# Squares of the first weights on ScalarE, the first root on VectorE, and the third weights a third of a unit later, in an attention, FFT and MLP kernel on one core

## The chip, the core and the metric

The kernel runs on one core of one Trainium2 chip. The metric is device time in microseconds (us), the median of several executions. The engines of the core work in parallel, each through its own queue and in order: TensorE (PE, matmuls), VectorE (DVE), ScalarE (ACT), GpSimd (POOL) and SyncE (SP), whose queue issues the DMA transfers. A wait at the head of a queue holds up everything behind it on that engine.

## The reference: what is computed

```python
x = attn_out.transpose(0, 2, 1, 3).reshape(4, 576, 512)       # 8 heads of 64
X = np.fft.fft(np.fft.fft(x, axis=1), axis=2)
u = x + np.real(X)
un = (u - u.mean(-1, keepdims=True)) / np.sqrt(u.var(-1, keepdims=True) + 1e-6)
x = u + np.maximum(un @ w_ch1, 0.0) @ w_ch2                   # 512 -> 2048 -> 512
gate_pre = sum(conv_w[k] * xp[:, k:k + 576, :] for k in range(5))   # xp: x with 4 zeros ahead
out = (1 / (1 + np.exp(-gate_pre)) * (x @ w_val)) @ w_out
```

attn_out is the sum of two attentions over q, k, v (4 batches, 8 heads, 576 tokens, 64 wide): one over tokens averaged by fours, and one over a band of width |i-j| < 4. The five weight arrays come as 64-bit floats.

## The kernel before, in words

**Units.** The MLP and the gated convolution run over 12 units (b, j): batch b, and 192 of its 576 tokens, j = 0 to 2. A unit is `ln` (layernorm, lines 960 to 1033), `ph` (first product, L1106, 192 matmuls in 8 groups of 24), `hh` and `hl` (the f16 high and low half of the ReLU, by ACT L1110 and DVE L166), `pc` (second product, L1126, again 192), then five taps of the convolution (`W<-X,cw` or `tap<-X,cw`), `val` (the product with w_val, L1218), `gl` and `gh` (gate times value in two halves) and `out` (L1234). Products use three f16 passes: high by high, high by low, low by high. Only unit (0,0) is done in fp32 (L1068 and L1081), because the f16 halves of the weights do not exist yet.

**Weights.** A 64-bit weight arrives as two 32-bit words and is made an f32 by three integer operations on DVE (`to_f32`, lines L302 and L166; "words" below). The sum of squares of the array then gives a power of two as its scale (`pow2`), and `conv_w` makes a high half on ACT (L372) and a low half on DVE (L166, 128x1024). w_ch1 is `W1` (8 positions), w_ch2 is `W2` (8 positions), and w_val and w_out are the "third weights" (positions 16 to 19). The sum of squares of W1 comes from 64 bf16 matmuls of a block with itself (`gram`, L356), whose diagonal DVE adds up (`tr`, `ss`); for w_val it is squares on ACT and matmuls with ones (`cv`, L400), for w_out again a gram (`cv`, L356). The third weights' words arrive in tiles named `raw`, in slots that the attention of the next batch uses too; SP issues these transfers among the loads `v` of that attention, which wait for POOL's sums `vr` and `ptv`.

**Fourier.** While units (0,1) and (0,2) run, batch 1's attention and Fourier transform are done beside them: `ab` over features, `pp`, `pn` and `pq` over the sequence, the last of which DVE turns into `DS` and adds to X. Unit (1,0) starts with `ln(1,0)`, which needs these sums: `uc` (X less its mean), `sq`, the sum `st`, `vv`, the root `r` (seven operations), `uc<-uc,r`, and `uh` and `ul`, the f16 halves which `ph` reads.

**Order.** Every step is recorded with a position in units (`put`, `spread`; positions S_..., P_... in lines 52 to 80), some with a priority (`urgent`), and a scheduler then writes one queue for each engine. The changed constants are S_W1B (the last two W1 words), S_W3 (the third weights), P_T0 (taps, values and outputs of unit (0,0)) and ROOT_G (the units whose root is done by POOL). The root of the first unit is computed in `ln` (L1008 to L1025).

Of the kernel before, what the change touches and what calls it, by code (L numbers as in the profile page):

```python
# [51 lines left out]
S_W1B = -7.47  # L52
# [8 lines left out]
S_W3 = (1.02, 1.6)  # L61
# [6 lines left out]
P_T0 = ((0.4, 0.75), (0.8, 1.0), (1.3, 1.75))  # L68
# [11 lines left out]
ROOT_G = ((0, 0), (0, 1))  # L80
# [48 lines left out]
def attn_moe_kernel(ctx, tc, q_t, k_t, v_t, w1, w2, w_val, conv_t, w_out, c_feat, c_seq, c_band, c_eye, out):  # L129
# [121 lines left out]
    def total(cols, n, name, act=False):  # L251

        ps = pst("tot", [P, n])
        T.matmul(out=ps, lhsT=ones, rhs=cols, start=True, stop=True)
        if act:
            assert n == 1
            r = keep.tile([P, 1], F32, name="f2s_" + name)
            A.activation(out=r, in_=ps, func=AF.Copy, scale=float(DM))
            return r
        t = keep.tile([P, 1], F32, name="f2_" + name)  # L260
        V.tensor_reduce(out=t, in_=ps, axis=AX.X, op=ALU.add)
        r = keep.tile([P, 1], F32, name="f2s_" + name)
        V.tensor_scalar(out=r, in0=t, scalar1=float(DM), scalar2=None, op0=ALU.mult)
        return r
# [62 lines left out]
    def word_w(i):  # L327
        if i < 16:
            raw = raws.pop(i)
            n = 1024 // len(raw)  # L330
            pos = AT[i] if i < 8 else 8
            for z, x in enumerate(raw):
                last = to_f32(W[AT[i] + 1].bitcast(I32)[:, z * n:(z + 1) * n], x,
                       lambda g=gates if pos < 4 else gates1 if pos < 6 else gates2: g.pop(0) if len(g) > 1 else g[0])
            if pos == 7:
                gates2[:] = [last.ins]
            if i == 11:
                st[0]["worded"] = last
# [27 lines left out]
    def trace_w(key):  # L366
        return total(diagonal(gram[key], key), 1, key, key in ("w1", "w2"))
# [50 lines left out]
    def attn_steps(b):  # L418
# [63 lines left out]
        def dense(sp):  # L482
# [92 lines left out]
            def values(g, e):  # L575
# [37 lines left out]
                if not first:  # L613
                    A.activation(out=vw[g], in_=vw[g], func=AF.Square, accum_out=d["ssv"][:, g:g + 1])
# [61 lines left out]


# [8 lines left out]
        def lowres():  # L686
# [3 lines left out]

            for a in range(H // 2):
# [282 lines left out]
    def ln(b, j):  # L974
# [39 lines left out]
        r1 = tiny.tile([P, UT], F32, tag="r1", name="r1", bufs=2)
        for a, c in ((-0.703952253, 0.703952253 * 2.38924456), (-0.5, 1.5)):
            mul(e, r1, r0, r0)
            if e is G:
                mul(e, r1, r1, vv)
                e.tensor_scalar(out=r1, in0=r1, scalar1=a, scalar2=c, op0=ALU.mult, op1=ALU.add)
                mul(e, r0, r0, r1)  # L1020
            else:
                stt(e, r1, r1, a, vv, ALU.mult, ALU.mult)
                stt(e, r0, r1, c, r0, ALU.add, ALU.mult)
# [304 lines left out]
    def put(pos, f):  # L1328
        events.append((pos, len(events), f))
# [12 lines left out]
    put(S_G1[1], lambda: urgent(w1_scale, "S"))  # L1342
    spread([(1.0, lambda i=i: sumsq_w(i, "w2", i == 8, i == 15)) for i in range(8, 16)], *S_G2)
# [18 lines left out]
    assert S_N0 < S_W1B <= S_W2[0] and 4 / 17 < S_C0[0] and 8 / 17 < S_C1[0] and S_C1[1] <= 9 / 17  # L1362
# [81 lines left out]
```

## Time and profile before

| what | value |
|---|---|
| median of 3 runs | 730.36 us (728.93 to 731.26) |
| profiled execution | 730.66 us, of which the span of the trace is 728.9 us |
| PE busy | 687.0 us (94%) |
| DVE busy | 467.0 us (64%) |
| ACT busy | 316.9 us (43%) |
| POOL busy | 122.5 us (17%) |
| mean granted TensorE clock | 0.967 of full speed |

Times of the trace count from the first instruction of the span; 1.76 us of the profiled execution lie outside it. A line of the trace gives start, duration, engine, source line, operation, output and input tiles and shapes, and in brackets how long the engine stood idle before and what released it. Shares of busy time are averages over the whole span; what a stage can gain is read from the waits of that stage.

### The profile page before, as it was taken

The page shows a single profiled execution, that of the slowest core. Times are in us where ns is not written, and L with a number is a line of the kernel's source. Part 1 is how long each engine was busy: PE and PEld are TensorE (multiplying, and loading weights), DVE is VectorE, ACT ScalarE, POOL GpSimd, SP SyncE. Part 2 cuts the span into 40 slices and gives each one's busy share as a digit, 9 for nine tenths or more (in the row PEclk, how much of TensorE's full clock was granted, in tenths as well). Part 3 has the DMA queues.
Part 4 walks back from the last instruction along what each step waited for, and adds up shares of the span by engine and source line. Part 5 has one row for each costly group of instructions (what it writes and reads, how often), then busy time and mean ns, then how long its engine had stood idle before and what let it go on. Part 6 is the DMA issues. An engine that isn't in the chain of part 4 may idle for free.

```text
span 728.9 us, 18440 instructions
## 1 busy us (share of the span) xinstructions
PE 687.0 (94%) x7849; PEld 599.6 (82%) x7849; DVE 467.0 (64%) x978; ACT 316.9 (43%) x980; POOL 122.5 (17%) x167
## 2 busy tenths in 40 slices
PE   8588799989899988999999999999999999999997
PEld 4346599988778967868898898789899989999895
DVE  4885699987978776466976725829635572633324
ACT  1674224686355336756423835644413232322212
POOL 0400054025222022330202107003100010000000
PEclk9758999989999999999999999999999999999999
DMA  9964314623422301240230001003000000000001
GB/s 240 377 228 167 101 66 167 155 82 129 144 60 83 100 1 39 61 136 16 77 103 2 26 15 43 17 1 97 18 16 16 1 16 16 1 17 2 30 2 44
DMA packets 27574, 53.01 MB, mean 73 GB/s; under 512 B 2112, under 2 KB 16320, under 8 KB 26468
## 3 DMA queue, kind: packets, MB, share of 16 engines
q1 hardware_dynamic: 27492, 51.84, 22.1%
q8 instruction: 61, 1.00, 0.6%
q14 instruction: 21, 0.17, 0.1%
HBM read 45.34 MB, written 8.26 MB: 74 GB/s over the span
## 4 chain that ended last, share of the span: by engine, by line
PE 67%; DVE 18%; ACT 6%; DMA 5%; POOL 2%; issue 1%; SPq 1%; POOLq 0%; ACTq 0%; DVEq 0%
PE pc L1126 19%; PE ph L1106 18%; DVE W L166 6%; PE out L1234 5%; PE val L1218 5%; ACT dP L565 3%; DMA v<-in_v_dram 2%; PE po L751 2%; PE ab L863 1%; DVE fF L835 1%; PE dO L606 1%; PE ph L1068 1%; DVE X L172 1%; PE sc L701 1%; PE pc L1081 1%
## 5 line engine op out<-in xcount | busy, mean ns | idle before, releaser
L1106 PE MATMUL ph<-uh,W 128*128 128x192 f16 x1408 | 195.3, 246 | 1.6 <-ACT uh L1032 1.6
L1106 PEld LDWEIGHTS <-W 128*128 128x128 f16 x2112 | 175.1, 98 | 7.9 <-issue 6.4
L1106 PE MATMUL ph<-ul,W 128*128 128x192 f16 x704 | 173.2, 246 | 0.0
L1126 PE MATMUL pc<-hh,W 128*128 128x192 f16 x1232 | 171.6, 247 | 0.9 <-ACT hh L1110 0.9
L1126 PEld LDWEIGHTS <-W 128*128 128x128 f16 x1848 | 154.2, 98 | 10.4 <-issue 8.4
L1126 PE MATMUL pc<-hl,W 128*128 128x192 f16 x616 | 151.3, 247 | 3.9 <-DVE hl L166 3.9
L166 DVE SCALAR_TENSOR_TENSOR hl<-ph,hh 128x384 f16<-128x384 f32 x88 | 48.2, 550 | 91.3 <-ACT hh L1110 91.2
L1110 ACT ACTIVATE hh<-ph 128x384 f16<-128x384 f32 x88 | 43.1, 494 | 103.0 <-PE ph L1106 99.9
L166 DVE SCALAR_TENSOR_TENSOR W<-X,cw,W 128x192 f32<-128x192 f32 x160 | 60.2, 432 | 0.9 <-ACT W L1181 0.7
L1218 PE MATMUL val<-yy,W 128*128 128x192 f16 x576 | 52.9, 246 | 0.1
L1218 PEld LDWEIGHTS <-W 128*128 128x128 f16 x576 | 47.9, 98 | 2.4 <-issue 0.6
L565 ACT ACTIVATE dP<-dS,dmx 128x64 f32<-128x64 f32 x160 | 48.1, 337 | 0.7 <-PE dPT L586 0.3
L1234 PE MATMUL out<-W,gh 128*128 128x512 f16 x144 | 45.6, 379 | 0.0
L565 ACT ACTIVATION_READ_ACCUMULATOR dP<-dS,dmx 128x1 f32 x160 | 36.8, 230 | 0.0
L166 DVE SCALAR_TENSOR_TENSOR W<-W,W 128x1024 int32<-128x1024 int32 x24 | 29.0, 1232 | 0.1
L715 ACT ACTIVATE E<-sc,nm 72x144 f32<-72x144 f32 x64 | 23.6, 378 | 9.4 <-POOL vr L172 4.7
L1234 PE MATMUL out<-W,gl 128*128 128x512 f16 x72 | 27.3, 379 | 0.0
L1081 PE MATMUL pc<-h,W 128*128 128x192 f32 x128 | 26.2, 357 | 0.0
L1234 PEld LDWEIGHTS <-gh 128*128 128x128 f16 x144 | 14.1, 98 | 13.7 <-issue 0.2
L1126 PE MATMUL pc<-hh,Wz 128*128 128x192 f16 x176 | 25.2, 246 | 0.0
L1068 PE MATMUL ph<-u,W 128*128 128x192 f32 x128 | 24.0, 345 | 1.0 <-DVE u L996 1.0
L1126 PEld LDWEIGHTS <-Wz 128*128 128x128 f16 x264 | 22.2, 98 | 2.7 <-issue 0.2
(243 smaller groups left out, 1208.1 us busy)
## 6 DMA issues: line engine op xcount, KB each, us to landing
W<-in_moe_w_ch_dram SPq DMA_DIRECT2D x12, 1024.0 KB
v<-in_v_dram SPq DMA_DIRECT2D x32, 144.0 KB
out_dram<-osb SPq DMA_DIRECT2D x17, 256.0 KB
vw<-in_v_dram SPq DMA_DIRECT2D x16, 256.0 KB
X<-in_q_dram SPq DMA_DIRECT2D x6, 576.0 KB
kT<-in_k_dram SPq DMA_DIRECT2D x4, 582.0 KB
X<-in_moe_w_ch_dram SPq DMA_DIRECT2D x2, 1024.0 KB
raw<-in_moe_w_ch_dram SPq DMA_DIRECT2D x4, 512.0 KB
```

Source lines behind the costliest of these rows:

```text
L166: return eng.scalar_tensor_tensor(out=out, in0=in0, scalar=scalar, in1=in1, op0=op0, op1=op1)
L172: return eng.tensor_tensor(out=out, in0=a, in1=b, op=ALU.add)
L565: A.activation(out=s_[:, z, a], in_=pss[par][:, z, a], func=AF.Exp, scale=SCALE, bias=mx[:, par, z, a:a + 1], accum_out=su[:, par, z, a:a ...
L715: A.activation(out=E[:, qc], in_=ps[:, qc], func=AF.Exp, scale=SCALE / 16, bias=nm[:, qc:qc + 1], accum_out=su[:, qc:qc + 1],)
L751: T.matmul(out=po[par * 64:par * 64 + 64], lhsT=d["vr"][:, kc, (a % 2) * 4 + (a // 2) * 2 + par], rhs=ets[par][:, kc], start=(kc == 0), st ...
L1068: i = T.matmul(out=ps[:, e], lhsT=W[AT[kc * 2 + m // 8] + 1][:, o:o + 128], rhs=u()[:, kc, :], start=(kc == 0), stop=(kc == 3))
L1081: T.matmul(out=c["ps"][m // 2][:, m % 2], lhsT=W[9 + g][:, o:o + 128], rhs=hs[g // 2][:, g % 2, e, :], start=(kk == 0 and m % 2 == 0), sto ...
L1106: T.matmul(out=ps[:, e], lhsT=w1_ap(pw, kc, 2 * g + e), rhs=uh[px][:, kc, :], start=(t == 0), stop=(t == 11))
L1110: A.activation(out=h_, in_=ps, func=AF.Relu)
L1126: T.matmul(out=ps[m // 2][:, m % 2], lhsT=w2_ap(pw, kk, m), rhs=x[px][:, e, :], start=(kk == 0 and (pw, px) == (0, 0) and m % 2 == 0), sto ...
L1218: T.matmul(out=ps[:, e], lhsT=wv_ap(pw, kc, 2 * mh + e), rhs=m_["y"][px][:, kc, :], start=(t == 0), stop=(t == 11))
L1234: T.matmul(out=ps, lhsT=(gh, gl)[px][:, kc, t * 128:(t + 1) * 128], rhs=wo_ap(pw, kc), start=(n == 0), stop=(n == 11))
```

## The change

- W1's last two word positions are no longer recorded at S_W1B, after the first unit's mean is subtracted, but with the other six.
- W1's sum of squares is taken by eight ACT activations with an accumulated output, right behind `sq` of unit (0,0), in place of 64 gram matmuls, and its total adds eight columns.
- The first unit's root is done by DVE, recorded at S_R0 = 0.8, in place of POOL.
- The third weights are recorded at 1.35 to 1.95 in place of 1.02 to 1.6, and unit (0,0)'s taps, values and outputs about a third of a unit later.
- The squares of v (`vw`) of batches 1 to 3 are recorded in another function; their place in ACT's queue is in effect the same.

```diff
-S_W1B = -7.47
-S_W3 = (1.02, 1.6)
+S_W3 = (1.35, 1.95)
-P_T0 = ((0.4, 0.75), (0.8, 1.0), (1.3, 1.75))
+P_T0 = ((0.75, 0.93), (1.0, 1.3), (1.6, 2.0))
-ROOT_G = ((0, 0), (0, 1))
+ROOT_G = ((0, 1),)
+S_R0 = 0.8
...
 def total(cols, n, name, act=False):
...
-            assert n == 1
             r = keep.tile([P, 1], F32, name="f2s_" + name)
-            A.activation(out=r, in_=ps, func=AF.Copy, scale=float(DM))
+            A.activation(out=tiny.tile([P, n], F32, tag="p2t", name="p2t"), in_=ps, func=AF.Copy, scale=float(DM), accum_out=r)
...
 def word_w(i):
...
-                       lambda g=gates if pos < 4 else gates1 if pos < 6 else gates2: g.pop(0) if len(g) > 1 else g[0])
-            if pos == 7:
-                gates2[:] = [last.ins]
+                       lambda g=gates if pos < 4 else gates1 if pos < 8 else gates2: g.pop(0) if len(g) > 1 else g[0])
...
 def sumsq_w(i, key, first, last):
+        if key == "w1":
+            if first:
+                gram[key] = keep.tile([P, 8], F32, name="ss_" + key)
+            behind(st[0]["sq"].ins, lambda: A.activation(
+                out=spare.bitcast(BF16)[:, 0:1024], in_=W[AT[i] + 1], func=AF.Square,
+                accum_out=gram[key][:, i % 8:i % 8 + 1]))
+            return
...
-            behind(st[0]["st2"].ins if i < 8 else None, lambda: T.matmul(
-                out=gram[key], lhsT=blk, rhs=blk, start=(first and c == 0), stop=(last and c == 7)))
+            T.matmul(out=gram[key], lhsT=blk, rhs=blk, start=(first and c == 0), stop=(last and c == 7))
...
 def ln(b, j):
...
-        vv = tiny.tile([P, UT], F32, tag="r2", name="vv", bufs=2)
+        vv = tiny.tile([P, UT], F32, tag="r2", name="vv", bufs=2) if not head else keep.tile([P, UT], F32, name="vv0")
         e = G if (b, j) in ROOT_G else V
...
+        if head:
+            st[0]["r"], st[0]["root"] = r0, root
+            return
+        root()
...
+    put(S_R0, lambda: st[0]["root"]())
-    for r, f, p in ((W1_ORDER[:6], w_in, S_W1), (W1_ORDER[:4], w_out_, S_C0), (W1_ORDER[4:], w_out_, S_C1), (range(8, 16), w_in2, S_W2)):
+    for r, f, p in ((W1_ORDER, w_in, S_W1), (W1_ORDER[:4], w_out_, S_C0), (W1_ORDER[4:], w_out_, S_C1), (range(8, 16), w_in2, S_W2)):
-    for i in W1_ORDER[6:]:
-        put(S_W1B, lambda i=i: urgent(lambda: w_in(i), "S"))
```

The table of positions tells little of the queues, so three places are shown as the scheduler wrote them. Numbers behind a name tell buffers of one tile apart.

DVE, in unit (0,1): the words of the third weights (`W_122<-raw`, `W_123<-raw`) stand between the steps of the unit; `hl` at the end is the low half that the third group of the second product waits for. Before, from the operation that reads the second `raw` tile:

```order
L302 TENSOR_SCALAR W_122<-raw 128x512
L720 RECIPROCAL lsu<-lsu 72x2 x2
L166 SCALAR_TENSOR_TENSOR W_122<-raw,W_122 128x512
L708 TENSOR_REDUCE nm<-sc 72x2
L166 SCALAR_TENSOR_TENSOR W_122<-raw,W_122 128x512
L302 TENSOR_SCALAR W_122<-raw 128x512
L172 TENSOR_TENSOR sq<-sq 128x384
L708 TENSOR_REDUCE nm<-sc 72x2
L166 SCALAR_TENSOR_TENSOR W_122<-raw,W_122 128x512
L166 SCALAR_TENSOR_TENSOR hl<-ph,hh 128x384
```

With the change, from the same operation:

```order
L301 TENSOR_SCALAR W_122<-raw 128x512
L731 TENSOR_SCALAR lsu<-lsu 72x2
L732 RECIPROCAL lsu<-lsu 72x2
L166 SCALAR_TENSOR_TENSOR W_122<-raw,W_122 128x512
L732 RECIPROCAL lsu<-lsu 72x2
L166 SCALAR_TENSOR_TENSOR hl<-ph,hh 128x384
```

Three operations on raw words, two maxima `nm` and a sum `sq` that stood ahead of `hl` now stand behind it.

SP's queue at the same place: `v` are loads for batch 1's attention. Before:

```order
L189 DMA raw<-in_moe_w_val_dram 128x1024
L187 DMA v_1828<-in_v_dram 72x2x256
L189 DMA v_1863<-in_v_dram 72x2x256
L189 DMA v_1864<-in_v_dram 72x2x256
L189 DMA v_1871<-in_v_dram 72x2x256
L189 DMA v_1872<-in_v_dram 72x2x256
L189 DMA raw<-in_moe_w_val_dram 128x1024 x2
```

With the change:

```order
L189 DMA raw<-in_moe_w_val_dram 128x1024
L187 DMA v_1765<-in_v_dram 72x2x256
L189 DMA v_1800<-in_v_dram 72x2x256
L189 DMA v_1801<-in_v_dram 72x2x256
L189 DMA v_1808<-in_v_dram 72x2x256
L189 DMA raw<-in_moe_w_val_dram 128x1024
L189 DMA v_1809<-in_v_dram 72x2x256
L189 DMA raw<-in_moe_w_val_dram 128x1024
```

The second `raw` now stands ahead of the last of these loads.

DVE, at the start of unit (1,0), from the last sums of batch 1's Fourier part on. Before, the whole way to `uc<-X,st` and `sq`:

```order
L166 SCALAR_TENSOR_TENSOR DS<-pp,ivx_1_2033,qs 128x289 x2
L172 TENSOR_TENSOR X<-X,DS 128x289 x2
L172 TENSOR_TENSOR uc<-X 128x384
L172 TENSOR_TENSOR uc<-uc 128x192
L166 SCALAR_TENSOR_TENSOR X<-pc_3087,iv_1559,X 128x2x192
L996 TENSOR_TENSOR uc<-X,st 128x768
L554 TENSOR_REDUCE dmx<-dS 128x4 x2
L166 SCALAR_TENSOR_TENSOR X<-pc_3088,iv_1559,X 128x2x192
L172 TENSOR_TENSOR sq<-sq 128x384
L172 TENSOR_TENSOR sq<-sq 128x192
```

With the change, two pieces of the same stretch:

```order
L166 SCALAR_TENSOR_TENSOR DS<-pp,ivx_1_1970,qs 128x289 x2
L172 TENSOR_TENSOR X<-X,DS 128x289 x2
L166 SCALAR_TENSOR_TENSOR W_121<-W_122,s_wv,W_121 128x1024
L169 TENSOR_TENSOR tr<-cv,eye 128x128
L172 TENSOR_TENSOR uc<-X 128x384
L166 SCALAR_TENSOR_TENSOR W_121<-W_122,s_wv,W_121 128x1024
L366 TENSOR_REDUCE ss_wo<-tr 128x1
L172 TENSOR_TENSOR uc<-uc 128x192
```

```order
L166 SCALAR_TENSOR_TENSOR W_123<-X,cw,W_123 128x192 x2
L166 SCALAR_TENSOR_TENSOR gl<-tap,gh 128x2x192
L166 SCALAR_TENSOR_TENSOR W_123<-X,cw,W_123 128x192
L166 SCALAR_TENSOR_TENSOR tap<-tap,val 128x384
L166 SCALAR_TENSOR_TENSOR W_123<-X,cw,W_123 128x192
L169 TENSOR_TENSOR uc<-uc,r_2955 128x768
L166 SCALAR_TENSOR_TENSOR W_123<-X,cw,W_123 128x192 x4
L559 TENSOR_REDUCE dmx<-dS 128x8 x2
L166 SCALAR_TENSOR_TENSOR gl<-tap,gh 128x2x192
L166 SCALAR_TENSOR_TENSOR W_123<-X,cw,W_123 128x192 x2
L1050 TENSOR_TENSOR ul<-uc,uh 128x768
```

The conversions of w_val (and, between the two pieces, the trace, the scale and the two conversions of w_out), unit (0,0)'s two products `tap<-tap,val` and its two `gl`, and 13 taps of unit (0,1) stood ahead of `DS` before, and now stand between `DS` and `ul`. The two `X<-pc` that stood there are ahead of `DS` now, and `yy<-X`, which stood ahead of `ul`, too.

## Rows read from the trace of the kernel before

**Rows 1.** Stretches: bounds, us; busy (x count) PE, PEld, DVE, ACT, POOL; clock, DMA.

```profile
91.40:150.00 58.60, 58.43 (x583) 56.14 (x587) 57.91 (x79) 26.11 (x81) 19.80 (x25) 0.97 0.42 125
150.00:163.70 13.70, 11.50 (x151) 10.57 (x139) 10.40 (x18) 13.13 (x42) 2.33 (x6) 0.75 0.27 89
186.90:262.50 75.60, 74.23 (x810) 66.18 (x810) 59.00 (x141) 33.23 (x87) 12.69 (x18) 0.98 0.28 87
262.50:277.60 15.10, 10.56 (x164) 7.61 (x162) 13.29 (x25) 6.31 (x23) 4.54 (x6) 1.00 0.05 19
400.00:728.90 328.90, 323.69 (x3728) 294.76 (x3725) 167.84 (x387) 117.84 (x312) 32.55 (x42) 1.00 0.06 21
```

**Rows 2.** Timeline of PE, unit (0,0): start, us, line, operation, count, idle before.

```profile
99.80 3.83 PE L356 MATMUL gram<-W 128*128 128x128 bf16 x64
...
153.25 1.11 PE L606 MATMUL dO<-PT,vw 64*64 64x58 f32 x16 [2.20 <-ACT PT L592]
154.29 6.55 PE L1081 MATMUL pc<-h,W 128*128 128x192 f32 x22
...
161.85 1.89 PE L1081 MATMUL pc<-h,W 128*128 128x192 f32 x10
```

**Rows 3.** One line's instructions, L614 on ACT: min/median/max ns.

```profile
L614 ACT ACTIVATE vw<-vw x9: 628/1058/1161, 145.9 to 447.0; 128x1024 f32<-128x1024 f32 x6, 128x512 f32<-128x512 f32 x3
```

**Rows 4.** Timeline of DVE: base sums, and W1's last two words.

```profile
64.69 2.76 DVE L172 TENSOR_TENSOR X<-X,base 128x576 f32<-128x576 f32 x4 [8.67 <-ACT X L612]
...
92.58 4.62 DVE L166 SCALAR_TENSOR_TENSOR W<-W,W 128x1024 int32<-128x1024 int32 x4
```

**Rows 5.** Timeline of SP, loads between the first and second raw tile.

```profile
166.80 10.03 SPq L189 DMA_DIRECT2D v<-in_v_dram  x4
```

**Rows 6.** Timeline of DVE, the second raw tile and the third hl.

```profile
181.51 0.81 DVE L302 TENSOR_SCALAR W<-raw 128x512 int32<-128x512 int32 x1 [3.13 <-DMA raw<-in_moe_w_val_dram]
...
186.28 0.54 DVE L166 SCALAR_TENSOR_TENSOR hl<-ph,hh 128x384 f16<-128x384 f32 x1
```

**Rows 7.** Timeline of PE at the same place.

```profile
186.87 0.24 PE L1126 MATMUL pc<-hl,W 128*128 128x192 f16 x1 [2.56 <-DVE hl L166]
```

**Rows 8.** Timeline of DVE: what the change moves, where it stood.

```profile
222.86 1.30 DVE L166 SCALAR_TENSOR_TENSOR W<-W,s_wv,W 128x1024 f16<-128x1024 f32 x1 [1.62 <-ACT W L372]
...
228.94 0.14 DVE L248 TENSOR_SCALAR s_wo<-p2b 128x1 int32<-128x1 int32 x1
...
229.80 1.01 DVE L166 SCALAR_TENSOR_TENSOR tap<-tap,val 128x384 f32<-128x384 f32 x2
...
236.15 0.54 DVE L166 SCALAR_TENSOR_TENSOR gl<-tap,gh 128x384 f16<-128x384 f32 x1
...
293.06 2.74 DVE L166 SCALAR_TENSOR_TENSOR W<-X,cw,W 128x192 f32<-128x192 f32 x8
```

**Rows 9.** Timeline of DVE, end of ln(1,0).

```profile
266.64 0.61 DVE L166 SCALAR_TENSOR_TENSOR X<-pc,iv,X 128x384 f32<-128x384 f32 x1
...
276.61 1.01 DVE L166 SCALAR_TENSOR_TENSOR yy<-X,s_y,yy 128x768 f16<-128x768 f32 x1
277.60 0.96 DVE L1033 TENSOR_TENSOR ul<-uc,uh 128x768 f16<-128x768 f32 x1
278.48 1.28 DVE L554 TENSOR_REDUCE dmx<-dS 128x8 f32<-128x512 f32 x2
```

**Rows 10.** Timeline of PE: last pq, st, 12 out, first ph with ul.

```profile
262.23 0.29 PE L888 MATMUL pq<-seq,AL 96*128 96x289 f16 x1
...
270.55 0.56 PE L990 MATMUL st<-sq,ones 128*128 128x192 f32 x2 [2.49 <-DVE sq L172]
270.95 0.38 PE L1234 MATMUL out<-W,gh 128*128 128x512 f16 x1
...
273.33 0.38 PE L1234 MATMUL out<-W,gh 128*128 128x512 f16 x1
...
279.68 0.25 PE L1106 MATMUL ph<-ul,W 128*128 128x192 f16 x1
```

More of the change, by code (lines that the diff above doesn't have):

```diff
@@ L366, in trace_w @@
     def trace_w(key):
-        return total(diagonal(gram[key], key), 1, key, key in ("w1", "w2"))
+        if key == "w1":
+            return total(gram[key], 8, key, True)
+        return total(diagonal(gram[key], key), 1, key, key == "w2")
     def conv_w(i, s, eng):
@@ L612, in values @@
                     A.activation(out=X[:, x, :, PAD + q0:PAD + q0 + nt], in_=pos[x], func=AF.Copy)
-                if not first:
-                    A.activation(out=vw[g], in_=vw[g], func=AF.Square, accum_out=d["ssv"][:, g:g + 1])
             def pool_qk(z, w):
@@ L675, in dense, with squares @@
             steps.extend(lr + v1)
+            def squares():
+                for g in range(len(GROUPS)):
+                    A.activation(out=vw[g], in_=vw[g], func=AF.Square, accum_out=d["ssv"][:, g:g + 1])
+            if not first:
+                d["squares"] = squares
         def scale_x():
@@ L689, in _ @@
                 d["base"] = sm.tile([P, 4, SD], F32, tag="base", name="base", bufs=1)
+            if b:
+                steps.append((0.1, d["squares"]))
             for a in range(H // 2):
@@ L1001, in ln @@
         sq = l_t("sq", [P, 4, UT])
-        A.activation(out=sq, in_=uc, func=AF.Square)
+        i = A.activation(out=sq, in_=uc, func=AF.Square)
+        if head:
+            st[0]["sq"] = i
         ps = colsum(sq, sq)
-        vv = tiny.tile([P, UT], F32, tag="r2", name="vv", bufs=2)
+        vv = tiny.tile([P, UT], F32, tag="r2", name="vv", bufs=2) if not head else keep.tile([P, UT], F32, name="vv0")
         e = G if (b, j) in ROOT_G else V
-        if e is G:
+        if e is G or head:
             A.activation(out=vv, in_=ps, func=AF.Copy, bias=1e-6)
@@ L1011, in ln, with root @@
         r0 = keep.tile([P, UT], F32, name="r00") if head else tiny.tile([P, UT], F32, tag="r0", name="r0", bufs=2)
-        e.tensor_scalar(out=r0.bitcast(I32), in0=vv.bitcast(I32), scalar1=-0.5, scalar2=float(0x5F1FFFF9),
-                        op0=ALU.mult, op1=ALU.add)
         r1 = tiny.tile([P, UT], F32, tag="r1", name="r1", bufs=2)
[L1015 to L1023, printed above, removed]
+        def root():
+            e.tensor_scalar(out=r0.bitcast(I32), in0=vv.bitcast(I32), scalar1=-0.5, scalar2=float(0x5F1FFFF9),
+                            op0=ALU.mult, op1=ALU.add)
+            for a, c in ((-0.703952253, 0.703952253 * 2.38924456), (-0.5, 1.5)):
+                mul(e, r1, r0, r0)
+                if e is G:
+                    mul(e, r1, r1, vv)
+                    e.tensor_scalar(out=r1, in0=r1, scalar1=a, scalar2=c, op0=ALU.mult, op1=ALU.add)
+                    mul(e, r0, r0, r1)
+                else:
+                    stt(e, r1, r1, a, vv, ALU.mult, ALU.mult)
+                    stt(e, r0, r1, c, r0, ALU.add, ALU.mult)
+        if head:
+            st[0]["r"], st[0]["root"] = r0, root
+            return
+        root()
         r1 = r0
-        if head:
-            st[0]["r"] = r1
-            return
         mul(V, uc, uc, r1.unsqueeze(1).to_broadcast([P, 4, UT]))
@@ L1361, in attn_moe_kernel @@
     assert S_LD[1] <= S_T0[0] and S_L1 <= S_W1[0] and S_T0[1] <= S_S0[0] and S_S0[1] <= S_F0[0] and S_F0[1] <= S_N0
-    assert S_N0 < S_W1B <= S_W2[0] and 4 / 17 < S_C0[0] and 8 / 17 < S_C1[0] and S_C1[1] <= 9 / 17
+    assert S_N0 <= S_W2[0] and 4 / 17 < S_C0[0] and 8 / 17 < S_C1[0] and S_C1[1] <= 9 / 17
     assert S_S0[1] <= S_END <= S_F0[0] and 1 <= S_W3[0]
```

## Prediction, made before the changed kernel was run

> **What bounds the kernel now.** I read the busy times by stretch first [rows 1]. From 400 us to the end PE works 323.69 of 328.9 us: there the kernel is bound by PE, the order of the work is hardly changed, and nothing can be won or lost but a few tenths. What the change can move lies before 300 us, where PE waits at four places. I read those from PE's timeline and then, for each, from the queue that released it.
>
> At 151 us PE stands idle for 2.20 us, waiting for PT of batch 1's attention, and then runs slowly: 22 fp32 matmuls take 6.55 us, 0.298 each, where the next ten take 1.89, 0.189 each [rows 2]. The stretch has a mean granted clock of 0.75 [rows 1], so TensorE fell to the lower of its levels (1.2 in place of 2.4 GHz) for a part of it. That costs 22 x 0.109 = 2.4 us.
>
> At 186.87 PE waits 2.56 us for the third `hl` [rows 7]. DVE's queue shows why: it stood still for 3.13 us in front of the second `raw` tile of w_val, read that at 181.51, and came to `hl` at 186.28, ending at 186.82, 4.77 us after it had begun on `raw` [rows 6]. The raw transfer is late because SP issues it behind four `v` loads that take 10.03 us to be issued, since POOL frees their tiles slowly [rows 5].
>
> From 186.9 to 262.5 PE is idle for 75.60 - 74.23 = 1.4 us [rows 1]. At 262.5 begins ln(1,0): from the end of the last `pq` (262.52) to the end of `ul` (278.56) DVE needs 16.0 us [rows 9, 10], and PE works only 10.56 of 15.10 us [rows 1], waiting 2.49 us for `sq` among others [rows 10]. In this stage, and only here, DVE sets the pace, and that decides the change.
>
> **The change part by part** (minus is earlier). The sum is made against the profiled execution, 730.66 us, which is 0.3 above the median of the runs.
>
> *W1's last two words* go ahead of the base sums. They take 4.62 us and two operations more of some 1.3 [rows 4], 5.9 together; DVE stands idle for 8.67 us just there [rows 4]. That covers them with 2.7 to spare; without the cover the first Fourier part would be late by up to 5.9.
>
> *The gram* leaves PE: 64 matmuls, 3.83 us [rows 2], right ahead of the first `ph` of unit (0,0), with PE busy 58.43 of 58.60 us around it [rows 1]. So all of it is on the path: -3.8. Eight squares of 128x1024 on ACT take its place; the same form, with its sum, takes 1.06 us on L614 [rows 3], so 8.5. ACT is busy 26.11 of 58.60 us there [rows 1] and PE's `h` evictions stand among them, so an eviction may be late by one square, 1.06, of which I count nothing since two groups are in flight (upper end +1.1). The Trainium skill (ScalarE: Activation LUTs, Rules for kernel authors) speaks against this: it says that products belong on VectorE, which is faster for them. Here it would be worse by the rows: DVE is busy 57.91 of those 58.60 us [rows 1], and by the 1.2 us of its 128x1024 operations [rows 4] the rule would add 9.6 us to the engine that has no room.
>
> *The first root on DVE* adds seven operations of 128x192; a tap of that size costs 0.34 [rows 8], so 2.5 to 3.5 us. Against that, 5.9 us of words are gone from DVE behind `u`, so W2's words end some 3 us earlier than before, and POOL, which computes W1's scale, is free of the first root. Both scales come earlier. Then the halves of W2, which ACT converts in front of PT, are out of the way sooner, and I take the 2.20 wait and the 2.4 of low clock that follow it to vanish. Lower end: nothing of the 4.6; upper end all. Together unit (0,0) ends 3.8 + 2.2 + 2.4 = 8.4 us earlier.
>
> *The raw wait* does not move with it, because its transfer waits for POOL and SP. Two things help. Behind the `raw` read, the queue now has one more word operation, three small ones and then `hl`: 0.81 + 0.67 + about 0.2, so `hl` starts 1.7 us after `raw` and not 4.77: -3.1. And the second `raw` passes one `v` load of the four: between 0 and 10.03 / 4 = 2.5 us earlier; I take 1.3, the middle, as nothing tells which of the four waits. So PE goes on 4.4 us earlier than at 186.87 before (3.1 to 5.6), and 4 us of the lead of 8.4 are lost there.
>
> *From there to the last pq.* 48 `val` and the 16 matmuls of w_out's gram leave this stretch, 42 `pc` enter it (they stood behind `pq`): 22 matmuls fewer, at 328.9 / 3728 = 0.088 each [rows 1], -1.9, of which I take 1.7 as the gram's are shorter. The 1.4 us of idle time stood where DVE converted the third weights, which leave. So `pq` ends 4.4 + 1.7 + 1.4 = 7.5 us earlier, at 255.0.
>
> *What DVE must do between pq and ul.* This is the part that costs. In one queue, ahead of `ul`, stand now: four conversions of 1.25 (1.30 alone) [rows 8], 5.0; eleven small steps of the scales and the trace, 0.14 each [rows 8], 1.4 with some overlap; two products tap with val, 1.01 as a pair [rows 8]; two `gl`, 0.54 each [rows 8], 1.0; 13 taps of 0.343 (2.74 for eight) [rows 8], 4.5; two `dmx`, 1.28, that stood behind `ul` [rows 9], 1.2 with overlap. Gone from there are two `X<-pc` of 0.6 and one `yy` of 0.9 [rows 9], 2.1. Net 14.1 - 2.1 = 12.0. DVE had 15.10 - 13.29 = 1.8 us of idle time in this stretch [rows 1], most of it between dependent steps; the new work fills some 1.2 of that. So the way is longer by 10.8 us (9.9 to 12): `ul` ends at 255.0 + 16.0 + 10.8 = 281.8.
>
> *What PE meets.* It had its first `ph` with `ul` at 279.68 [rows 10], 1.1 after `ul` was there, as it had `val` to do. Now `val` is done long before and PE waits: +10.8 - 1.1 = 9.7. The 12 `out` of unit (0,0), which filled the old wait from 270.95 to 273.71 [rows 10], come later, since their `gl` do: 2.8 us of PE's work that no longer hides. So the price is 9.7 + 2.8 = 12.5, the lead 7.5.
>
> **Sum:** -7.5 + 12.5 = +5.0, so 730.66 + 5.0 = 735.7, and 5.3 above the median. Behind this point the order is nearly the old one and PE is full, so it stays to the end. A clock that falls is not in the sum: the old stage held 1.00 through waits of 2.49 and less [rows 1, 10].
>
> **Rivals.**
>
> *Late third weights cost nothing (no change).* If POOL and SP get through the `v` loads sooner because batch 1's attention is earlier by up to 8.4 us, the wait for `raw` [rows 6, 7] is gone: then the whole lead of 8.4 + 2.6 = 11.0 comes through, and 14.1 at `pq`; net -1.6, 729.1. Half of it gives 732.3. For it: the loads wait for POOL, and POOL is idle for most of these stretches [rows 1]. Against: 10.03 us of issue for four loads [rows 5] is the loads' own chain, which starts only where the first `raw` does.
>
> *Faster.* The same, and the 12 `out` find a place where PE would stand anyway: the price is 9.7, the lead 14.1, net -4.4, 726.3. It decides from a lead of 12 us on: whether the third `hl` is ready when PE comes to it.
>
> *The clock falls.* PE is idle for some 14 of the 27 us between `pq` and `ul`, in stretches longer than the old 2.49. After 2.20 at 151 it fell, and that cost 2.4 [rows 2]. Then 735.7 + 2.4 = 738.1, or 740.5 if it happens twice. The Trainium skill (TensorE: Matmul & The Clock Gate, Part 1) says that the throttled level is the default and that activity lifts it, by which this rival would be the rule. The rows show both: a fall after 2.20, none after 2.49.
>
> *The change does not do what it says.* If the squares or the root came late, W1's scale would be late and the low halves of W1 with it. ACT has 30 us free there [rows 1] for 8.5 us of work, so I give it little; it would cost up to 3 and stay within the range.
>
> **How the numbers follow.** About 0.3%, 2.2 us, is what a measurement of this kernel can tell from no change. The sum as it stands, with or without the fall of the clock: 0.55, all of it slower. No change, 728.2 to 732.5: 0.20. Faster: 0.25, more than the rows alone would give, because the lead is known to 3 us only and each microsecond of it counts fully. The forecast is the likeliest, 735.7. The range goes down to 725.5 for the faster case, and up to 741 for a lead of 6.2 (3.1 at the raw tile), a price of 13.7 and one fall of the clock: 730.66 + 7.5 + 2.4 = 740.6. The likeliest case alone has 733 to 740.5.
>
> **What would show it.** Right: no gram at 100 us; no wait for PT at 151 and a full clock behind it; the third `hl` near 182; the last `pq` near 255; then DVE without a gap for 27 us, PE idle for more than 12 us of them, and the first `ph` with `ul` near 282, later than 279.68 though everything ahead is earlier. Wrong: the last `pq` ahead of 251, or `ul` less than 23 us behind it. If `pq` is on time and `ul` too but the end is not 5 us later, PE made up for it behind 300 us, which I exclude.

## The result, and the profile after

| | before | after |
|---|---|---|
| median of five runs each, on one chip | 728.93 us (728.20 to 731.26) | 734.31 us (733.22 to 734.92) |
| ratio, 95% interval | | 1.0070 (1.0049 to 1.0092): slower by 5.4 us |
| profiled execution, its span | 730.66, 728.9 | 733.22, 731.4 |
| mean granted clock | 0.967 | 0.965 |

The two traces show only 2.6 of these 5.4 us: before's profiled execution lies 1.7 above its median, after's is the lowest of its five. The other 2.8 cannot be placed on a line.

I read after in the order in which the prediction read before. The stretches first, with the columns of [rows 1], their bounds moved to after's own events:

```profile
91.40:150.00 58.60, 57.42 (x576) 55.29 (x577) 55.80 (x82) 39.17 (x112) 10.25 (x19) 0.97 0.47 146
150.00:163.70 13.70, 12.52 (x161) 11.26 (x160) 12.25 (x23) 12.54 (x40) 4.63 (x3) 1.00 0.02 4
177.20:252.30 75.10, 71.66 (x784) 63.07 (x784) 52.28 (x114) 26.51 (x74) 15.40 (x22) 1.00 0.31 94
252.30:260.00 7.70, 2.23 (x21) 1.99 (x21) 6.81 (x15) 2.58 (x3) 1.66 (x2) 0.89 0.00 0
260.00:270.00 10.00, 8.06 (x79) 6.82 (x78) 9.32 (x25) 8.64 (x30) 2.56 (x2) 0.57 0.01 2
270.00:279.50 9.50, 5.51 (x121) 4.67 (x119) 9.50 (x22) 3.93 (x18) 1.30 (x2) 0.96 0.01 2
400.00:731.40 331.40, 326.12 (x3780) 296.86 (x3776) 170.00 (x390) 117.62 (x312) 33.82 (x44) 1.00 0.06 21
```

From 400 us on, PE is as full as it was. The clock of the second stretch, the end of unit (0,0), went from 0.75 to 1.00. The new weak place is the 27.2 us from the last `pq` to `ul`: DVE is busy for 25.63 of them (6.81 + 9.32 + 9.50), PE for 15.80, and for ten of them its mean granted clock is 0.57. In before this way took 16.0 us, and the 15.1 of them in [rows 1] had 1.00.

PE's timeline at the same places as [rows 2, 7, 10] (in brackets: idle time ahead, and its releaser; `...` stands for rows left out):

```profile
148.78 5.04 PE L1098 MATMUL pc<-h,W 128*128 128x192 f32 x30
153.75 0.68 PE L611 MATMUL dO<-PT,vw 64*64 64x58 f32 x16
154.36 0.59 PE L1098 MATMUL pc<-h,W 128*128 128x192 f32 x2
...
177.22 0.24 PE L1143 MATMUL pc<-hl,W 128*128 128x192 f16 x1 [1.20 <-DVE hl L166]
...
181.21 0.56 PE L1002 MATMUL st<-sq,ones 128*128 128x192 f32 x2 [2.02 <-DVE sq L172]
...
258.85 0.59 PE L254 MATMUL tot<-ss_wo,ones 128*128 128x1 f32 x2 [4.86 <-DVE ss_wo L366]
...
263.51 0.98 PE L1002 MATMUL st<-sq,ones 128*128 128x192 f32 x2 [1.94 <-DVE sq L172]
264.28 4.05 PE L1235 MATMUL val<-yy,W 128*128 128x192 f16 x24
268.54 2.14 PE L1235 MATMUL val<-yy,W 128*128 128x192 f16 x24
...
279.49 0.32 PE L1123 MATMUL ph<-ul,W 128*128 128x192 f16 x1 [2.47 <-DVE ul L1050]
...
287.44 0.39 PE L1251 MATMUL out<-W,gh 128*128 128x512 f16 x1
...
289.83 0.38 PE L1251 MATMUL out<-W,gh 128*128 128x512 f16 x1
```

Unit (0,0) ends at 154.95 in place of 163.74, and `dO` no longer waits for PT. The third `hl` lets PE go on at 177.22, not 186.87. Then the lead is spent. `ss_wo` costs 4.86 us of idle time, 24 `val` take 4.05 us where the next 24 take 2.14 (the granted clock is low there), and the first `ph` with `ul` starts at 279.49, 0.2 ahead of [rows 10]. Twelve `out` that had been done before that `ph` still lie ahead.

DVE's timeline, to compare with [rows 6, 9]:

```profile
175.48 0.43 DVE L301 TENSOR_SCALAR W<-raw 128x512 int32<-128x512 int32 x1 [3.75 <-DMA raw<-in_moe_w_val_dram]
...
176.63 0.54 DVE L166 SCALAR_TENSOR_TENSOR hl<-ph,hh 128x384 f16<-128x384 f32 x1
...
253.75 1.78 DVE L172 TENSOR_TENSOR X<-X,DS 128x289 f32<-128x289 f32 x2
255.46 1.27 DVE L166 SCALAR_TENSOR_TENSOR W<-W,s_wv,W 128x1024 f16<-128x1024 f32 x1
...
263.62 3.21 DVE L166 SCALAR_TENSOR_TENSOR W<-W,s_wo,W 128x1024 f16<-128x1024 f32 x2
...
268.61 0.36 DVE L169 TENSOR_TENSOR r<-r 128x192 f32<-128x192 f32 x1
...
274.86 1.39 DVE L166 SCALAR_TENSOR_TENSOR W<-X,cw,W 128x192 f32<-128x192 f32 x4
276.17 1.27 DVE L559 TENSOR_REDUCE dmx<-dS 128x8 f32<-128x512 f32 x2
...
278.49 0.95 DVE L1050 TENSOR_TENSOR ul<-uc,uh 128x768 f16<-128x768 f32 x1
```

Conversions (`W<-W,s_wv`, `W<-W,s_wo`), taps and `dmx` stand between `X<-X,DS` and `ul`, as the order said.

### The profile page after: what moved, and what is told of

Its sections match the earlier page's. It is cut to its first block, busy times and chain, and to the rows that moved or that the text cites. A ratio compares the mean times of both kernels' runs of the same rounds, so it can differ in the third digit from the quotient of the medians.

```text
span 731.4 us, 18333 instructions
## 1 busy us (share of the span) xinstructions
PE 682.0 (93%) x7785; PEld 594.6 (81%) x7785; DVE 468.5 (64%) x983; ACT 326.3 (45%) x998; POOL 111.7 (15%) x158
## 5 line engine op out<-in xcount | busy, mean ns | idle before, releaser
L166 DVE SCALAR_TENSOR_TENSOR W<-X,cw,W 128x192 f32<-128x192 f32 x160 | 61.7, 440 | 1.2 <-ACT W L1198 1.0
L1235 PE MATMUL val<-yy,W 128*128 128x192 f16 x576 | 54.8, 251 | 0.0
L1251 PEld LDWEIGHTS <-gh 128*128 128x128 f16 x144 | 14.1, 98 | 13.7 <-issue 0.2
L1198 ACT ACTIVATE W<-X,cw 128x192 f32<-128x192 f32 x40 | 15.6, 451 | 20.9 <-DVE X L166 19.0
```

What stands on the lines that cost most here:

```text
L166: return eng.scalar_tensor_tensor(out=out, in0=in0, scalar=scalar, in1=in1, op0=op0, op1=op1)
L1198: A.activation(out=m, in_=x, func=AF.Copy, scale=w)
L1235: T.matmul(out=ps[:, e], lhsT=wv_ap(pw, kc, 2 * mh + e), rhs=m_["y"][px][:, kc, :], start=(t == 0), stop=(t == 11))
L1251: T.matmul(out=ps, lhsT=(gh, gl)[px][:, kc, t * 128:(t + 1) * 128], rhs=wo_ap(pw, kc), start=(n == 0), stop=(n == 11))
```

## The experiments

Each kernel was run beside before on the same chip, in three groups of runs. "Against before" is its median less that of before in its own group of runs (728.6 to 729.7); the change itself is at +5.4. All are told against one of three sets of positions: **old** (before's), **new** (the change's), and **middle**, which I chose between them. "Structure" means the rest of the change: words, squares, root.

**1 and 2: the two halves of the change.** The first kernel is the change with before's positions, the second is before with the change's positions.

```diff
-S_W3 = (1.35, 1.95)
+S_W3 = (1.02, 1.6)
-P_T0 = ((0.75, 0.93), (1.0, 1.3), (1.6, 2.0))
+P_T0 = ((0.4, 0.75), (0.8, 1.0), (1.3, 1.75))
```

> The changed kernel with the third weights and unit (0,0)'s taps, values and outputs recorded at the old positions (1.02 to 1.6; 0.4 to 1.75); squares, root and words as changed. Theory (the pile of DVE work in ln(1,0) costs some 12 us, the rest of the change earns 8 to 10): the third hl stays at about 176.6 and the conversions go back ahead of DS, so the way from the last pq to the end of ul is 16 to 18 us and the time is 720 to 725, faster than before by 4 to 9. Rival A (the gains of the first 180 us are lost again anyway, in the DVE-bound stretch before pq or in a transfer): 727 to 731. Rival B (squares on ScalarE or the root on VectorE cost the time, not the move): 733 to 736, as the changed kernel.

> The kernel before with the two new positions alone. Theory: the wait for the third hl at 187 stays as it was, the pile is there (about 27 us from the last pq to the end of ul), and without the lead of the other parts the time is 736 to 741, slower than the changed kernel. Rival A: the move by itself is neutral because the stretch before pq gains what ln(1,0) loses: 728 to 732. Rival B: 727 to 731, the move not being the cause.

Structure alone: 734.25, ratio 1.0069 (1.0040 to 1.0098), against before +5.1. Positions alone: 736.45, 1.0092 (1.0061 to 1.0122), +7.3. The second came as my theory had it (27 us from `pq` to `ul`, as forecast). The first did not: my theory said that without the late work the lead would come through. Its time lies in the range of rival B, and the way from `pq` to `ul` is 19.6 us, not 16 to 18. The halves don't add up (+5.1 and +7.3 make +5.4), and each alone is slower. In the first kernel `ul` ends 2.2 us ahead of after's and 1.4 ahead of before's, with the 12 `out` done, and still the end is late. PE's timeline of it shows where:

```profile
310.18 0.71 PE L713 MATMUL sc<-qkT 64*72 64x144 f32 x4 [2.86 <-ACT E L727]
...
353.47 0.24 PE L1143 MATMUL pc<-hl,Wz 128*128 128x192 f16 x1 [2.01 <-DVE hl L166]
```

Its stretch behind the first of these waits:

```profile
310.00:320.00 10.00, 9.82 (x73) 7.48 (x74) 6.41 (x16) 4.80 (x15) 4.58 (x6) 0.83 0.43 109
```

`sc` (the scores of batch 2's attention) waits for `E` of ACT for 2.86 us. In before the same wait is 0.52:

```profile
311.41 0.71 PE L701 MATMUL sc<-qkT 64*72 64x144 f32 x4 [0.52 <-ACT E L715]
```

Behind it the clock is 0.83, which is 1.7 us of full speed lost in ten. The change touches neither operation; the scheduler gave the queues another order. What `E` waits for can be followed back through the queues of ACT, SP, POOL and ACT again:

```profile
296.63 0.20 ACT L723 ACTIVATE nm<-nm 72x2 f32<-72x2 f32 x1 [3.40 <-DVE nm L720]
...
298.78 1.27 SPq L189 DMA_DIRECT2D vw<-in_v_dram  x2
...
304.57 0.73 POOL L172 TENSOR_TENSOR vr<-v 72x256 f32<-72x256 f32 x1 [7.76 <-DMA v<-in_v_dram]
...
309.30 0.38 ACT L727 ACTIVATE E<-sc,nm 72x144 f32<-72x144 f32 x1 [4.86 <-POOL vr L172]
```

ACT stands still for 3.40 us ahead of `nm`, a maximum that DVE makes, and its square of `vw` comes behind that. SP issues the next `vw` at 298.78, when the square is done, and the `v` loads behind it. POOL's sum `vr` waits for `v`, and `E` for `vr`: 4.86 us here, 2.28 in before. So one late row at the head of ACT's queue reaches PE some 13 us later. This is read from the traces; no run moved that row alone.

**3: only the third weights back.** The change with S_W3 old, P_T0 new.

```diff
-S_W3 = (1.35, 1.95)
+S_W3 = (1.02, 1.6)
```

> The changed kernel with only the third weights back at 1.02 to 1.6; unit (0,0)'s taps, values and outputs stay at the new positions. By the queue only one product tap with val stands in ln(1,0) then, and no conversion. Theory (any DVE work between DS and ul is the cost, the conversions with what depends on them being most of it): 720 to 726. Rival (the late taps, values and outputs are what costs, 48 val and 12 out that fill no wait): 731 to 735.

735.18, 1.0084 (1.0054 to 1.0115), +6.0: my theory fell again, and the time is the rival's. The way from `pq` to `ul` shrank from 27.2 to 17.9 us and `ul` ended 5.2 earlier than after's, but all of that was lost later, with 12 `out` and 48 `val` late and a new wait in PE's timeline:

```profile
293.92 1.12 PE L591 MATMUL dPT<-eye,dP 128*128 128x128 f32 x4 [2.53 <-ACT osb L1269]
```

**4: positions in the middle.** The full structure, with both positions between old and new.

```diff
-S_W3 = (1.35, 1.95)
+S_W3 = (1.15, 1.75)
-P_T0 = ((0.75, 0.93), (1.0, 1.3), (1.6, 2.0))
+P_T0 = ((0.5, 0.8), (0.9, 1.1), (1.4, 1.8))
```

> The changed kernel with both positions between old and new (third weights 1.15 to 1.75; taps 0.5 to 0.8, values 0.9 to 1.1, outputs 1.4 to 1.8). By the queue ln(1,0) holds no conversion, no tap and no product. Theory: the time has a step and no slope, set by whether the work falls before or behind DS: 720 to 725, as with the old positions. Rival (later is dearer in proportion): 726 to 730.

**724.25**, 0.9932 (0.9908 to 0.9955), -5.0: faster than both kernels, the best found. PE's timeline of it:

```profile
268.60 0.38 PE L1251 MATMUL out<-W,gh 128*128 128x512 f16 x1
273.22 0.24 PE L1123 MATMUL ph<-ul,W 128*128 128x192 f16 x1 [0.67 <-DVE ul L1050]
...
303.63 0.71 PE L713 MATMUL sc<-qkT 64*72 64x144 f32 x4 [0.42 <-ACT E L727]
```

`ul` is 5.4 us earlier than before's, the last of the 12 `out` is done ahead of it, and the wait of `sc` is short. The table below suggests that all three have to hold at once. The time is in my theory's range, but the theory's ground for it, that the old positions would be as fast, had already fallen with the first kernel.

**5 and 9: DVE's work between pq and ul, by itself.** The fourth kernel with one operation of `ln(1,0)` repeated, 11 times and 6 times in all, with the same inputs, so that the output stays as it is. That puts 8.8 and 4.4 us of DVE work into the disputed stretch.

```diff
-        i = V.tensor_tensor(out=uc, in0=x, in1=ps.unsqueeze(1).to_broadcast([P, 4, UT]), op=ALU.subtract)
+        for _ in range(11 if (b, j) == (1, 0) else 1):
+            i = V.tensor_tensor(out=uc, in0=x, in1=ps.unsqueeze(1).to_broadcast([P, 4, UT]), op=ALU.subtract)
```

> The version with the middle positions (724.25 us before), with one operation of ln(1,0), X less its mean on DVE (128x768, 0.95 us), done eleven times in a row in place of once; the value is the same. It puts 10 x 0.88 = 8.8 us of DVE work between the last pq and ul and changes nothing else ahead of it. Theory (DVE work at this place is paid in full, since PE has no other work there): 8 to 10 us more, and 1 to 2.5 for a fall of the clock: 732 to 736. Rival (PE has slack behind it, and the time of the changed kernel comes from the order of later work): 725 to 729.

> As the pile test, with six executions of the operation in place of eleven: 4.4 us of DVE work more between the last pq and ul of the middle version. Theory (paid in full, and the excess over 8.8 us that eleven cost comes from falls of the clock): 728 to 731. Rival (slack for the first few microseconds, all the cost behind them): 724 to 726. Rival (a step: any delay there costs the same 12 to 13): 736 to 738.

8.8 us: 737.21, 1.0104 (1.0065 to 1.0142), +7.5, which is 12.5 more than the fourth kernel. 4.4 us: 730.75, 1.0052 (1.0025 to 1.0079), +2.1, 7.1 more. The first lies above every range that I gave, the second in my theory's. The time rose by what was put in and by 2.7 to 3.7 us more. `ul` moved by 9.4 and 4.3, hardly more than was put in; the rest came behind it. In PE's timeline of the kernel with 4.4 us:

```profile
269.64 0.98 PE L1002 MATMUL st<-sq,ones 128*128 128x192 f32 x2 [4.18 <-DVE sq L172]
...
313.17 0.71 PE L713 MATMUL sc<-qkT 64*72 64x144 f32 x4 [2.78 <-ACT E L727]
```

Its stretches, with the clock:

```profile
260.00:270.00 10.00, 4.44 (x69) 2.90 (x70) 8.26 (x14) 4.82 (x27) 1.18 (x2) 0.50 0.01 2
...
310.00:320.00 10.00, 7.22 (x46) 5.30 (x44) 3.57 (x9) 3.34 (x12) 6.69 (x9) 0.83 0.43 115
```

Beside the extra stand a lower clock in the stage (the fourth kernel has 0.83 in 260 to 270) and a longer wait of `sc`: 0.42 became 2.78. Lateness ahead of it does not explain that wait: in the seventh and eighth kernels `ul` ends about as late (283.0 and 277.3), and `sc` waits 0.54 and 0.37. The repeats also gave the scheduler another order behind `ul`. ACT now takes the gates' `tanh` ahead of its square of `vw` and waits for DVE there:

```profile
299.97 0.84 ACT L1221 ACTIVATE W<-W 128x768 f32<-128x768 f32 x1 [3.43 <-DVE W L166]
```

The wait is 3.44 in the fifth kernel and 3.17 in the twelfth. In the fourth that `tanh` stands behind the square, and the chain told under the first kernel starts earlier. So the repeats changed two things, and what they show for work between `pq` and `ul` by itself is that `ul` moves by its length.

**6 and 12: POOL takes the third weights' low halves.** The change, and the fourth kernel, with the four positions given to POOL.

```diff
-LO_G = ()
+LO_G = (16, 17, 18, 19)
```

> The changed kernel with the low halves of the third weights made by POOL in place of DVE; positions as changed. In DVE's queue the four conversions leave ln(1,0), and the scheduler puts the 13 taps and the two dmx behind ul too: some 11 us less between pq and ul; 48 val and 12 out stay late. Theory: 722 to 728. Rival (as undoing the move gave nothing, the work in ln(1,0) is not what holds it up): 732 to 736.

> The middle version with the low halves of the third weights made by POOL: 5 us less DVE work ahead of pq, 4 ACT copies more. Theory (DVE is not the bound there now): 722 to 727, no gain to speak of. Rival (the stretch before pq is bound by DVE): 718 to 721.

With the new positions: 732.90, 1.0056 (1.0027 to 1.0085), +3.2, in the rival's range. With the middle ones: 732.65, 1.0068 (1.0045 to 1.0092), +4.0, above the ranges of both my theory and the rival, of which neither had it slower than before. In the first of them DVE lost four conversions, but the way to `ul` shrank only from 27.2 to 22.8. DVE's timeline:

```profile
264.59 1.51 DVE L1029 TENSOR_SCALAR r<-vv 128x192 int32<-128x192 int32 x1
266.14 1.04 DVE L169 TENSOR_TENSOR r<-r 128x192 f32<-128x192 f32 x1
...
268.27 2.17 DVE L169 TENSOR_TENSOR r<-r 128x192 f32<-128x192 f32 x1
```

And POOL's of the same kernel:

```profile
263.87 2.12 POOL L380 TENSOR_TENSOR W<-W,W 128x1024 f16<-128x1024 f32 x1 [3.29 <-issue]
265.95 1.01 POOL L172 TENSOR_TENSOR uc<-X 128x384 f32<-128x384 f32 x1
...
268.05 2.18 POOL L380 TENSOR_TENSOR W<-W,W 128x1024 f16<-128x1024 f32 x1 [0.42 <-ACT W L379]
```

The steps of the root, 0.26 and 0.36 in after, take 1.51, 1.04 and 2.17 us here, and each ends within 0.25 us of a POOL operation's end (265.99, 266.96, 270.23). The work taken from DVE came back as DVE's steps held up on the path. The Trainium skill (SBUF — State Buffer, Who interferes with whom) says that a DVE operation with two inputs in SBUF contends with a GpSimd operation that reads SBUF; for `r<-r` the rows agree. `r<-vv`, which was stretched as well, has one input. In the twelfth kernel the last `pq` itself is late (261.0 against 254.4), which I did not follow further.

**7: before, with the middle positions.** So that the fourth kernel's gain is not put down to its positions alone.

```diff
-S_W3 = (1.02, 1.6)
+S_W3 = (1.15, 1.75)
-P_T0 = ((0.4, 0.75), (0.8, 1.0), (1.3, 1.75))
+P_T0 = ((0.5, 0.8), (0.9, 1.1), (1.4, 1.8))
```

> The kernel before with the middle positions alone. If squares, root and words earn the 8.5 us by which unit (0,0) and (0,1) end earlier, this is 727 to 731, as the kernel before, and 3 to 6 slower than the middle version with them. If the middle positions alone made the gain, 722 to 726.

732.84, 1.0047 (1.0021 to 1.0074), +3.2. This is slower than either of my ranges had it. So at the middle positions the structure is worth -4.95 - 3.15 = -8.1 us, and the two intervals lie apart. At the old ones it is +5.1. At the new ones it is 5.4 - 7.3 = -1.9, which the intervals don't tell from nothing.

**8, 10 and 11: parts of the structure, and one position, in the fourth kernel.** The eighth has W1's gram back on PE; the tenth has only P_T0 old; the eleventh the first root back on POOL.

```diff
-        if key == "w1":
-            if first:
-                gram[key] = keep.tile([P, 8], F32, name="ss_" + key)
...
-            return total(gram[key], 8, key, True)
-        return total(diagonal(gram[key], key), 1, key, key == "w2")
+        return total(diagonal(gram[key], key), 1, key, key in ("w1", "w2"))
```

```diff
-P_T0 = ((0.5, 0.8), (0.9, 1.1), (1.4, 1.8))
+P_T0 = ((0.4, 0.75), (0.8, 1.0), (1.3, 1.75))
```

```diff
-ROOT_G = ((0, 1),)
+ROOT_G = ((0, 0), (0, 1))
```

> The version with the middle positions with W1's sum of squares from 64 gram matmuls on PE again; root on VectorE and words as changed. Theory (the 3.8 us of the gram are on PE's path and kept to the end): 727 to 730. Rival (the lead ends in a wait for batch 1's attention anyway): 723 to 726.

> The middle version with only unit (0,0)'s taps, values and outputs back at the old positions; the third weights stay at 1.15 to 1.75. DVE's queue differs from the old-position version in few rows; w_out's conversions stand as there. If the third weights' position is what makes the middle version fast, 723 to 727; if the taps, values and outputs are, or if the time comes with the queue order as a whole, 731 to 736, like the old positions.

> The middle version with the first root on POOL again. By the rows the root is needed only when the first product of unit (0,0) is scaled, and POOL's scale of W1 comes behind it. Theory (the root matters only through W1's scale, which had slack): 724 to 727. Rival (it delays the halves of W1 and so the f16 units): 727 to 731.

Gram on PE: 726.27, 0.9958 (0.9938 to 0.9978), -3.4. Root on POOL: 724.93, 0.9950 (0.9928 to 0.9972), -3.7. Both intervals overlap the fourth kernel's, so neither part is shown to be worth anything by itself. The first lies between the two ranges that I gave, the second in my theory's. P_T0 old: 734.36, 1.0075 (1.0047 to 1.0104), +5.8, as in the first kernel: moving unit (0,0)'s taps, values and outputs by up to a tenth of a unit makes 10.7 us.

**All kernels in one table**, from their profiled executions: the end of the last `pq`, of `ul`, the time from there to the end of the span, whether the 12 `out` came ahead of `ul`, and the longest wait of `sc` for `E` between 298 and 322 us.

| kernel | pq | ul | ul to end | out | sc wait |
|---|---|---|---|---|---|
| before | 262.5 | 278.6 | 450.3 | ahead | 0.52 |
| after | 252.3 | 279.4 | 452.0 | late | 0.81 |
| 1 structure, old positions | 257.6 | 277.2 | 455.4 | ahead | 2.86 |
| 2 positions alone | 253.6 | 280.2 | 452.7 | late | 2.24 |
| 3 S_W3 old | 256.3 | 274.3 | 458.6 | late | 0.97 |
| 4 middle | 254.4 | 273.2 | 447.2 | ahead | 0.42 |
| 5 middle, +8.8 us | 254.6 | 282.6 | 452.8 | ahead | 2.50 |
| 6 POOL, new | 252.4 | 275.3 | 453.8 | late | 0.91 |
| 7 before, middle | 261.8 | 283.0 | 448.4 | ahead | 0.54 |
| 8 gram on PE, middle | 258.6 | 277.3 | 447.4 | ahead | 0.37 |
| 9 middle, +4.4 us | 254.8 | 277.5 | 451.6 | ahead | 2.78 |
| 10 P_T0 old | 257.3 | 277.4 | 455.2 | ahead | 2.33 |
| 11 root on POOL, middle | 258.6 | 276.1 | 448.8 | ahead | 0.49 |
| 12 POOL, middle | 261.0 | 280.2 | 453.2 | ahead | 3.70 |

`ul` to the end takes 447.2 to 450.3 us wherever the outputs are ahead and `sc` waits less than 1 us, and 451.6 to 458.6 in every other kernel. That is a pattern over 14 traces, one execution each, and the gap between 450.3 and 451.6 is less than the 3 us by which before's five runs differ. No run removed the wait of `sc` alone. In the kernels 1, 5, 9, 10 and 12 ACT stands still for over 3 us ahead of its square of `vw`, for `nm` (1 and 10) or the `tanh` (5, 9 and 12); the second kernel has no such row, and its 2.24 stay unexplained.

## Why the prediction was right, and which of its steps were not

The forecast, 735.7 us, is 1.4 above the median, and the sign is as told. The way from `pq` to `ul` grew by 11.2 us and the lead was 10.3, but the 0.9 between them were taken up by the 1.1 us that `ul` had been ready ahead of its `ph`. In the traces it is the 12 `out` behind that make after longer. Two terms missed, and they partly cancel: the raw wait gave 5.2 us more lead than forecast, the stretch to the last `pq` 2.5 less.

*Words and squares.* Right. The eight squares, L351 in the view by source line:

```profile
L351 ACT ACTIVATE Wz<-W x8: 1042/1054/1057, 92.1 to 102.4; 128x1024 bf16<-128x1024 f32 x8
L351 ACT ACTIVATION_READ_ACCUMULATOR Wz<-W x8: 186/187/195, 93.0 to 103.3; 128x1 f32 x8
```

1.06 each as forecast, with 0.19 for reading the sum, which I had left out (1.5 us in all, free on ACT). The gram stood behind the first `ph` of unit (0,0), at 99.80, and not ahead of it as I wrote; PE is full on both sides, so the price is the same. The scale is ready at POOL at 106.6 and the first high half of W1 starts at 106.78, against 117.89. What the Trainium skill's rule (ScalarE: Activation LUTs, Rules for kernel authors) would have cost, squares on VectorE, was not run.

*Root, PT wait, clock.* Right in effect: unit (0,0) ends 8.8 earlier (forecast 8.4), with no wait and a full clock. Which part does it is open. In the eleventh kernel, with the root on POOL, the unit ends at 159.45 behind a wait for PT of 0.61, in the fourth at 155.34 without one; yet their times differ by 1.3 us only (-5.0 against -3.7), inside the interval, so the 4 us at this place are not shown to reach the end. Nor does the low clock always follow the wait: it is 2.20, 2.21 and 2.19 us in before, the seventh and the second kernel, and the 22 `pc` behind it take 6.55, 6.51 and 3.84.

*The raw wait.* This step failed: "4 us of the lead of 8.4 are lost there". `hl` started 9.65 earlier, not 4.4, so that of the lead of 8.8 nothing was lost on balance. SP's timeline shows why, beside [rows 5]:

```profile
162.60 0.36 SPq L189 DMA_DIRECT2D raw<-in_moe_w_val_dram  x1
163.06 0.34 SPq L187 DMA_DIRECT2D v<-in_v_dram  x1
163.50 6.52 SPq L189 DMA_DIRECT2D v<-in_v_dram  x3
170.27 0.36 SPq L189 DMA_DIRECT2D raw<-in_moe_w_val_dram  x1
```

The second `raw` was issued 6.67 earlier (170.27 against 176.94). Of that, 3.3 are the earlier start of the loads (163.50 against 166.80), whose cause stays open. Another 2.7 lie between the first and the third load. The third waits for a `ptv` of POOL, and that stood behind a sum which was long in before and short in after:

```profile
171.53 3.38 POOL L172 TENSOR_TENSOR vr<-vr,ptv 72x256 f32<-72x256 f32 x1
...
167.82 0.73 POOL L172 TENSOR_TENSOR vr<-vr,ptv 72x256 f32<-72x256 f32 x1
```

To pass the fourth load gave the last 0.65, not 1.3: it waited 0.8 us in before. The read came 6.0 earlier, and `hl` 1.15 behind it in place of 4.77 gave the other 3.6 (forecast 3.1). The rival "late third weights cost nothing" wanted the loads to come through sooner, and they did; but the wait for `raw` did not go. DVE still stood 3.75 us ahead of it and PE 1.20 ahead of `hl`, and the lead at `pq` became 10.3, not the rival's 14.1.

*To the last pq.* Forecast -3.1, measured -0.6 (75.03 us from the third `hl` to the end of `pq`, before 75.65). PE's busy time fell by 2.6, more than the 1.7 that I took. But its idle time rose from 1.37 to 3.44: what the order showed moving from ahead of `hl` to behind it now stands ahead of the last `sq` that `st` needs, and `st` waits 2.02 us at 181.21. I had counted the gain of that move and not who waits behind what was moved. So `pq` ended 10.3 earlier, forecast 7.5.

*DVE between pq and ul.* Right: 27.2 us, forecast 26.8. Of the single terms, the taps (0.35 to 0.41, three of them 0.58), `dmx` (1.27 for two) and the conversion of w_val (1.27) held; the two of w_out took 3.21 together, forecast 2.5. PE was idle for 11.4 us of the way, forecast more than 12.

*What PE meets.* The first `ph` with `ul` is 0.2 earlier, forecast 2.2 later, so this sign of being right did not come; the difference is the lead missed above. The 12 `out` are no longer hidden: 287.44 to 290.2, 2.8 us as forecast.

*The clock* was left out of the sum, as a rival. It did fall: 0.57 in 260 to 270. Most of that passed while PE would have waited for DVE anyway; but 280 to 290 us still had 0.89, some 1.1 us of full speed.

*The sum* from the traces is thus -0.2 + 2.8, and 2.5 is what the spans differ by; I had +5.0. That the two agree so well is in part chance. Up to batch 2's `sc`, 1.1 us of clock, 0.6 of further idle time and 27 fewer other matmuls are not in it (the last some 2.4 us at the prediction's 0.088 each, an estimate), and they nearly cancel. That the medians differ by 5.4 is more than these two traces show, so the forecast came near the median partly by luck. Nothing was made up behind 300 us, as my last paragraph had it: from about 310 us on the two traces differ by a constant.

*The theory behind the forecast* was that the late work alone is to blame. The first, third and tenth kernels refute that: with all of the work where it was, or the third weights alone, or the taps, values and outputs alone, the structure is as slow, through other waits. What the fifth and ninth show is only that work between `pq` and `ul` moves `ul` by its length. The row of the order behind the late `E` can be read, in the first and tenth kernels ACT's `nm` ahead of its square of `vw`; that it alone makes the time is not shown.

## What to carry to other kernels

Where a scheduler writes the queues, an edit's gain is known only together with the positions around it: take the edit, then move the neighbouring constants in small steps and read the next two late waits each time, before you judge it. Follow such a wait back through every queue: here one on ACT reached PE by way of SP and POOL. For every operation that the order shows moving behind another, look up who waits for it, not only what the other gains. And keep DVE's queue free between the last sums that a layernorm needs and its result, where, as in this kernel, PE has little else to do.

## What was not expected of the hardware

- 4.4 and 8.8 us more on DVE in a stage where PE waits cost 7.1 and 12.5 us: the clock in the stage was 0.50 and 0.62 where it had been 0.83, and the next attention's `sc` became late, the latter with another order on ACT.
- With POOL on the low halves, DVE operations of 0.26 to 0.36 us took up to 2.17, ending as POOL's ended; POOL needs 2.12 us for one low half, DVE 1.27.
- In after, PE idled 4.86 us ahead of 258.85, and the next 24 `val` took 4.05 us where 2.14 is the usual: the lower of the two levels, 1.2 GHz. The Trainium skill (TensorE: Matmul & The Clock Gate, Part 1) calls the throttled level the default from which activity lifts it; the rows agree here, while [rows 1, 10] with 2.49 us of idle time show no fall. A wait of 2.19 to 2.21 us for PT was followed by slow `pc` in two kernels and by fast ones in a third.
